# The last mode's transposed rows from products with its weights as stationary operand, and the first output units in another order

## The chip, the core and the metric

The kernel runs on one core of one Trainium2 chip. The metric is the device time of one execution in microseconds, as the median of several runs. All times inside an execution are counted from the start of the profiled span. PE is the matrix engine (its weight loads are told apart as PEld), DVE the vector engine, ACT the scalar engine, POOL and SP two further engines that here mainly issue DMAs.

## The reference, cut to what matters

```
# attention: 8 batches, 8 heads, 576 tokens, head size 64; causal window of 128 with a linear bias per head
attn = softmax(q @ k.T / 8 + bias)  (masked);   x = (attn @ v), heads side by side: [8, 576, 512]
# spectral mix, 64 modes, 512 channels
X  = rfft(x, axis=tokens)[:, :64]
Yr = Xr @ w_r[m] - Xi @ w_i[m];   Yi = Xr @ w_i[m] + Xi @ w_r[m]      # for every mode m: 512 x 512 weights
y  = irfft(Y, n=576);   u = x + y
out = u + relu(u @ w_ch)                                              # float32, [8, 576, 512]
```

The 64 pairs of 512 x 512 float32 weights are the bulk of what is read; the output is 9.4 MB.

## The kernel before, in words

The first part (up to some 138 us) is attention, done per batch and half of the heads; its output x stays on the chip, and its spectrum is laid down in XC, channels on the partitions, for each mode 32 columns (8 batches, real and imaginary parts, with signs). While it runs, and long after, POOL issues the loads of the mode weights, cast to bf16 in flight.

The second part goes through the modes as the weights come. Four modes make a group; their products (`nc.tensor.matmul(into[...], lhsT=XC[...], rhs=wq[t][a])`, L886) lie in four strips of 32 partitions of one PSUM tile, acc. The stationary operand is XC's 32 columns of a mode, the moving operand the 512 columns of its weights, and eight products make a mode: four channel quarters a for the real weights, four for the imaginary. A finished group is scaled, transposed and put into YT (`quad_end`), and YT is later turned into Z (the spectral rows per pair of batches) and ZW (the same times w_ch). In the shadow of the loads PE also projects the tokens by w_ch (XW) and adds the early modes' inverse transform (`project`, `augment`).

The last group (modes 60 to 63) is treated apart. Modes 60 to 62 go into a tile of their own, pa; `late_end` (L588 to L596) scales them into 96 rows of yq, patches those rows into Z by DMA, transposes them and puts the transposed columns into yT. Mode 63 comes last, in acc; its imaginary weights are loaded in three pieces, and PE does the real weights' four products, the transposes of the 96 rows, then the imaginary weights' four. After that stands the code that the change is about:

- ACT scales mode 63's 32 rows of acc into yq (L960), in two halves; PE transposes each half (L962), DVE copies it into yT (L964). A product of no use (L955) stands before, on PE.
- `late_channels` multiplies yT by w_ch (L601); ACT copies the result, in two halves, into yw, which lies in F's memory (L603).
- `patch` (L648) moves rows of yq into Z and of yw into ZW, one DMA per batch: for batches 0 and 1 partly on SP's queue, the others on POOL's, one after another.

Then the output is made in 18 units of two times 128 token rows (`units`; j = 0 to 3 are batches 0 and 1, j = 4 to 7 batches 2 and 3, j = 8 the last 64 tokens of batches 0 to 3, and so on). For a unit, mm gathers u @ w_ch (from XW and ZW: `begin`, `channels`), yy gathers u (from x and Z: `add_tokens`, `finish_tokens`); `activate` has ACT apply the relu to mm (L802), `finish` has DVE add yy and the relu (L842) into one of five buffers o, and SP issues the store (L844, L851). Units 1, 2 and 17 go in halves. mm and yy have two buffers each. Units 0 and 1 do not wait for patched rows of Z and ZW in all their parts: unit 0 takes the last group straight from yq and yw, through `last_rows` (L786). `with_tokens` has ACT copy unit 0's yy (L816), `finish_first` has DVE do relu and addition in one operation (L823).

The order on each engine is the order in which the code is written out: nothing is reordered by a scheduler. Waits are on other engines' counters and on DMA landings.

Of the kernel before, what the change touches and what calls it, by code (L numbers as in the profile page):

```python
# [10 lines left out]
FP32 = mybir.dt.float32  # L11
BF16 = mybir.dt.bfloat16
# [3 lines left out]
PSUM = bass.MemoryType.PSUM  # L16
# [4 lines left out]
P = 128  # L21
# [13 lines left out]
NC = 24  # L35
# [377 lines left out]
def kernel(  # L413
# [21 lines left out]
    XC = const.tile([P, 4 * NC * NM + 16 * NM], BF16, name="XC")  # L435
    ident = const.tile([P, P], BF16, name="ident")
# [24 lines left out]
    wq, homes, todo_w, again = {}, {}, [i for turn in turns for i in turn], []  # L461
# [108 lines left out]
    with ExitStack() as mctx:  # L570
# [8 lines left out]
        lctx, pctx = ExitStack(), ExitStack()  # L579
        lps = lctx.enter_context(tc.tile_pool(name="lps", bufs=1, side="right", space=PSUM))  # L580
        ps = pctx.enter_context(tc.tile_pool(name="fps", bufs=1, space=PSUM))
        heads, free, idle = {}, [], []
# [13 lines left out]
            nc.vector.tensor_copy(yT[:, :, rows], tr[:, :, rows])  # L596
            heads[LAST] = yq, yT

        def late_channels(zw, yT, yw, c):
            for et in range(4):  # L600
                nc.tensor.matmul(zw[:, c], lhsT=yT[:, et], rhs=wch[:, et, c],  # L601
                                 start=(et == 0), stop=(et == 3))
            nc.scalar.copy(yw[:, c], zw[:, c])  # L603

        def quad_end(acc, g):

# [57 lines left out]
        units = []  # L664
# [69 lines left out]
            nc.vector.tensor_copy(src[:, 1], ys[1])  # L734

        HALVES = (1, 2, len(units) - 1)
        mms, yys, rs = {}, {}, {}

        def pair(tag, slot=0):
            return heads[tag][slot].tile([P, 2, DM], FP32, tag=tag, name=tag)  # L740
# [68 lines left out]
        def finish_tokens(j):  # L809

            late_modes(yys[j][0], j, Z)

        def with_tokens(o, n):

            last_rows(yys[0][0], 0, heads["yq"], (n,))
            nc.scalar.copy(o[:, n], yys[0][0][:, n])  # L816

        def finish_first(o):

            (mm, mm_slot), (_, yy_slot) = mms.pop(0), yys[0]  # L820
            for n in range(2):
                last_rows(mm, 0, heads["yw"], (n,))
                nc.vector.scalar_tensor_tensor(out=o[:, n], in0=mm[:, n], scalar=0.0,  # L823
                                               in1=o[:, n], op0=ALU.max, op1=ALU.add)
                nc.sync.dma_start(out=out[n, :P], in_=o[:, n])
                if n == 0:
                    with_tokens(o, 1)
            del yys[0]
            idle.append(mm_slot)
            free.append(yy_slot)  # L830

        def finish(j):

            b, st = units[j]
            if j not in yys:
                take(j)
            add_tokens(j)
            finish_tokens(j)
            (yy, slot), r = yys.pop(j), rs.pop(j)
# [15 lines left out]
            free.append(slot)  # L855
# [4 lines left out]
        for g in range(NM // 4):  # L860
            if g == 0:
                lps.tile([P, 2, 4, P], BF16, tag="tr", name="tr")
            acc = (lps if g % 2 else ps).tile([P, DM], FP32, tag="acc", bufs=1, name="acc")
            if g == LAST:
                part_acc = ps.tile([P, DM], FP32, tag="pa", bufs=1, name="pa")
            for i in range(8):
                k = 8 * g + i
                if i == 6 and g == LAST:
                    pctx.close()
                    head = mctx.enter_context(  # L870
                        tc.tile_pool(name="hps", bufs=1, space=PSUM, reuse_waits="tile"))
                    heads.update(mm=[head], yy=[head])
                    idle.append(0)
                    free.append(0)
                    begin(0)
                    channels(0)
                    take(0)
                    add_tokens(0)
                    finish_tokens(0)
                now = turns.pop(0) if turns and spot[turns[0][0]] == k else []  # L880
                for a in range(4):
                    for t in now:
                        m, ri = t // 2, t % 2
                        c0 = (a // 2 * 2 * NC + 16 * (1 - ri) + a % 2 * 8) * NM + m
                        into = part_acc if g == LAST and m < NM - 1 else acc
                        nc.tensor.matmul(  # L886
                            into[32 * (m % 4) : 32 * (m % 4) + 32],
                            lhsT=XC[:, c0 : c0 + 31 * NM + 1 : NM], rhs=wq[t][a],
                            start=(ri == 0 and a == 0), stop=(ri == (m > 0) and a == 3),
                            tile_position=(0, 32 * (m % 4)),  # L890
                        )
# [7 lines left out]
                if k == K1:  # L899
# [45 lines left out]
            elif g == LAST - 1:  # L945
# [6 lines left out]
        zctx = ExitStack()  # L952
        zps = zctx.enter_context(tc.tile_pool(name="zps", bufs=1, space=PSUM))
        zl = zps.tile([P, DM], FP32, tag="z0", name="zl")
        nc.tensor.matmul(zl, lhsT=ident, rhs=wch[:, 0], start=True, stop=True)  # L955
        sides = (slice(0, DM // 2), slice(DM // 2, DM))
        trs = (lps.tile([P, 4, P], BF16, tag="tr", name="tr"),
               zps.tile([P, 4, P], BF16, tag="z1", name="tr1"))
        for i, c in enumerate(sides):
            nc.scalar.mul(yq[96:, c], acc[96:, c], 2.0 / S)  # L960
            for et in (2 * i, 2 * i + 1):
                nc.tensor.transpose(trs[i][:, et, 96:], yq[96:, et * P : (et + 1) * P],  # L962
                                    ident[96:, 96:])
            nc.vector.tensor_copy(yT[:, 2 * i : 2 * i + 2, 96:],  # L964
                                  trs[i][:, 2 * i : 2 * i + 2, 96:])
# [18 lines left out]
        begin(1)  # L984
        channels(1)
        channel_rows = partial(patch, rows=yw, dst=lambda b: ZW[:, b // 2, 1])
        channel_rows([(nc.sync, 0), (nc.sync, 1)] + [(nc.gpsimd, b) for b in range(2, B)])
        patch([(nc.gpsimd, 7)], yq, lambda b: Z[:, b // 2, 1], 6)

        assert not side  # L990
        finish_first(first)
        activate(1)
        finish(1)
        activate(2)
        for j in range(3, len(units)):
            activate(j)
            finish(j - 1)
# [31 lines left out]
```

## Time and profile before

| | us |
|---|---|
| median of 3 runs | 438.93 (438.69 to 439.68) |
| the profiled execution | 437.99 |
| its span | 436.1 |

| engine | busy, us | share of the span |
|---|---|---|
| PE | 316.2 | 73% |
| DVE | 184.5 | 42% |
| ACT | 162.3 | 37% |
| POOL | 90.2 | 21% |

The granted clock of PE was 0.862 in the mean of the span, and 1.00 from 396 to 431 us. HBM gave 162.53 MB and took 9.44 MB. The last weights' last product ended at 402.8; the first store was issued at 406.9; the DMA engines were busy with stores until 434.

How to read it: the page cuts the span into 40 slices of 10.9 us, and its DMA row gives the busy share of the 16 DMA engines in tenths. Its chain of waits lists what released what. The groups of instructions give a line, an engine, an operation, the tiles (out<-in), the shape and the mean length. The timeline gives start and length, how many instructions were merged into a row, and in brackets the idle time before it with what ended it.

### The profile page before, as it was taken

Reading aid. Unit: us, or ns where it says so; the run is one execution under the profiler, and the core shown is the slowest. Engines: PE = TensorE matmul, PEld = TensorE weight load, DVE = VectorE, ACT = ScalarE, POOL = GpSimd, SP = SyncE. Lnnn points to the kernel's source line nnn. Section 1 sums busy time; section 2 is a strip of 40 time slices with the busy share of each in tenths; the row PEclk is TensorE's granted clock in tenths of the full one; section 3 lists DMA queues with packets and bytes.
Section 4 is the critical chain, followed back from the end, with each engine's and each line's share of the span. In section 5 each row is a group of like instructions: output and inputs, shape, how many; then the busy total and the mean of one; then the engine's idle time right before and its main releaser. Section 6 shows DMA issues by size and latency. Waiting matters only on the chain.

```text
span 436.1 us, 8292 instructions
## 1 busy us (share of the span) xinstructions
PE 316.2 (73%) x3488; PEld 177.7 (41%) x3509; DVE 184.5 (42%) x332; ACT 162.3 (37%) x211; POOL 90.2 (21%) x170
## 2 busy tenths in 40 slices
PE   5589899979686635543442487999889999788982
PEld 4367677757565312111111133444434444334430
DVE  7789799887783301000000021322213233122684
ACT  6949899988681000000000011322222322102780
POOL 8701010103424002222112110101111110012600
PEclk9969999999999955555555569999999999989997
DMA  8999999999999999999999999999999999998598
GB/s 285 326 311 310 290 316 300 307 298 299 252 217 212 215 215 213 214 214 214 215 212 214 214 215 214 215 214 215 215 214 214 215 215 215 213 215 153 190 378 311
DMA packets 50453, 105.54 MB, mean 242 GB/s; under 512 B 4032, under 2 KB 21072, under 8 KB 50416
## 3 DMA queue, kind: packets, MB, share of 16 engines
q0 software_dynamic: 19440, 68.41, 77.9%
q1 hardware_dynamic: 30976, 36.60, 25.3%
q8 instruction: 27, 0.44, 0.4%
q14 instruction: 10, 0.08, 0.1%
HBM read 162.53 MB, written 9.44 MB: 394 GB/s over the span
## 4 chain that ended last, share of the span: by engine, by line
DMA 71%; PE 10%; DVE 8%; issue 5%; POOL 2%; ACT 1%; SPq 1%; DVEq 0%; POOLq 0%; ACTq 0%
DMA w<-in_moe_w_i_dram 42%; DMA wch<-in_moe_w_ch_dram 8%; DMA qr<-in_q_dram 7%; DMA vr<-in_v_dram 6%; DVE o L842 3%; DMA qr<-in_moe_w_i_dram 3%; PE my L702 2%; DMA vr<-in_moe_w_r_dram 2%; DMA kr<-in_k_dram 2%; DVE vb L246 1%; PE acc L886 1%; PE av L344 1%; POOL Z L648 1%; PE my L659 1%; DVE att L318 1%
## 5 line engine op out<-in xcount | busy, mean ns | idle before, releaser
L886 PE MATMUL acc<-w,XC 128*32 128x512 bf16 x456 | 80.3, 478 | 68.5 <-DMA w<-in_moe_w_i_dram 34.2
L886 PEld LDWEIGHTS <-XC 128*32 128x32 bf16 x508 | 38.4, 147 | 109.2 <-issue 82.8
L307 ACT ACTIVATE att<-sc 128x1024 bf16<-128x1024 f32 x64 | 64.1, 1032 | 9.7 <-PE sc L297 9.6
L636 ACT CAST ZW<-zw 128x512 bf16<-128x512 f32 x8 | 4.7, 585 | 142.9 <-PE zw L634 142.9
L344 PE MATMUL av<-vb,att 128*128 128x132 bf16 (+1 forms) x576 | 38.4, 217 | 13.3 <-DVE x L360 8.6
L344 PEld LDWEIGHTS <-att 128*128 128x128 bf16 x704 | 36.6, 98 | 18.7 <-DVE x L360 12.0
L608 DVE TENSOR_SCALAR yq<-acc 128x512 bf16<-128x512 f32 x14 | 9.6, 687 | 81.8 <-PE acc L886 81.8
L702 PE MATMUL my<-wch,xT 128*64 128x512 bf16 x288 | 34.5, 381 | 5.7 <-ACT x L733 4.2
L711 ACT CAST XW<-my 128x512 bf16<-128x512 f32 x36 | 19.3, 589 | 50.5 <-PE my L659 50.5
L683 DVE COPY xT<-tr 128x1024 bf16<-128x1024 bf16 x18 | 12.4, 692 | 54.9 <-PE tr L681 54.9
L269 ACT COPY qkT<-tp 128x1152 bf16<-128x1152 bf16 x30 | 33.5, 1116 | 4.1 <-PE tp L263 3.6
L491 POOL DMA_DIRECT2D w<-in_moe_w_r_dram x22 | 15.6, 710 | 72.1 <-PE acc L886 46.1
L491 POOL DMA_DIRECT2D w<-in_moe_w_i_dram x23 | 16.3, 709 | 64.1 <-PE acc L886 45.3
L297 PE MATMUL sc<-qkT 64*64 64x256 bf16 (+2 forms) x640 | 25.1, 263 | 4.8 <-ACT qkT L269 1.2
L360 DVE TENSOR_TENSOR x<-av,rec 128x640 bf16<-128x640 f32 x32 | 26.4, 825 | 1.1
L702 PEld LDWEIGHTS <-xT 128*64 128x64 bf16 x288 | 17.1, 109 | 21.5 <-issue 9.1
L246 DVE CAST vb<-vr 64x1024 bf16<-64x1024 f32 x32 | 22.6, 708 | 0.2
L733 ACT CAST x<-my 128x512 bf16<-128x512 f32 x18 | 10.5, 585 | 31.6 <-PE my L659 31.6
L297 PEld LDWEIGHTS <-qkT 64*64 64x64 bf16 x640 | 14.5, 109 | 19.1 <-issue 16.0
L734 DVE CAST x<-my 128x512 bf16<-128x512 f32 x18 | 12.4, 692 | 21.7 <-PE my L659 21.7
L842 DVE TENSOR_TENSOR o<-yy,r 128x1024 f32<-128x1024 f32 (+1 forms) x20 | 20.3, 1059 | 2.1 <-ACT r L802 1.9
L318 DVE TENSOR_TENSOR att<-att,mask 128x1024 bf16<-128x1024 bf16 x32 | 20.5, 682 | 0.0
(137 smaller groups left out, 424.7 us busy)
## 6 DMA issues: line engine op xcount, KB each, us to landing
w<-in_moe_w_i_dram POOLq DMA_DIRECT2D x23, 1024.0 KB, 36.2
w<-in_moe_w_r_dram POOLq DMA_DIRECT2D x22, 1024.0 KB, 35.6
qr<-in_q_dram SPq DMA_DIRECT2D x16, 576.0 KB, 7.9
kr<-in_k_dram SPq DMA_DIRECT2D x16, 576.0 KB, 7.9
w<-in_moe_w_r_dram POOLq DMA_DIRECT2D x16, 512.0 KB, 14.2
vr<-in_v_dram SPq DMA_DIRECT2D x56, 128.0 KB, 7.6
w<-in_moe_w_i_dram POOLq DMA_DIRECT2D x13, 512.0 KB, 24.0
out_dram<-o SPq DMA_DIRECT2D x13, 512.0 KB, 5.0
```

Of the source, the lines that this page charges most:

```text
L246: nc.vector.tensor_copy(self.vb[u % 2][row, :, :, :, W * half : W * half + D], src[row, :2])
L269: (self.nc.vector.tensor_copy if u < 2 and w == "q" else self.nc.scalar.copy)(dst.rearrange("q h (p j) -> q h p j", j=TPP), tp.rearrange(" ...
L297: nc.tensor.matmul(sc[64 * half : 64 * half + 64, e, j * 256 + c0 : j * 256 + c0 + n], lhsT=qkT[row, 1, h, k0 + j : k0 + P : 2], rhs=qkT[r ...
L307: self.nc.scalar.activation(self.att[u % 2][:, kt * 8 * P : (kt + 1) * 8 * P], sc.rearrange("p e n -> p (e n)"), AF.Exp, scale=1.0 / math. ...
L318: nc.vector.tensor_tensor(out=rows, in0=rows, in1=self.table[:, heads], op=ALU.mult)
L344: nc.tensor.matmul(bank[:, qt * W : qt * W + rhs[j].shape[1]], lhsT=att[:, o : o + P], rhs=rhs[j], start=(n == 0 and j == 0), stop=(n == l ...
L360: nc.vector.tensor_tensor(out=self.x[:, b, :, cs].rearrange("p t (h d) -> p h t d", h=2), in0=tiles[:, :, :, :D], in1=rec.unsqueeze(-1).br ...
L491: nc.gpsimd.dma_start(out=t.rearrange("p s a e -> p s (a e)"), in_=w[kinds.pop()][m : m + 2].rearrange("m (p a) e -> p m (a e)", a=4))
L702: nc.tensor.matmul(mm[ROWS[half]], lhsT=lhsT, rhs=wch[:, dt], start=(dt == 0), stop=False, skip_group_check=True,)
L711: nc.scalar.copy(XW[:, j, n], mms[n])
L842: nc.vector.tensor_tensor(out=o[:, c], in0=yy[:, c], in1=r[:, c], op=ALU.add)
L886: nc.tensor.matmul(into[32 * (m % 4) : 32 * (m % 4) + 32], lhsT=XC[:, c0 : c0 + 31 * NM + 1 : NM], rhs=wq[t][a], start=(ri == 0 and a == 0 ...
```

## The change

Mode 63's columns of yT are no longer transposed from acc. A new function, `last_columns`, multiplies them directly: the stationary operand is a 128 x 128 block of the mode's weights, the moving operand XC's 32 columns, and 32 such products (two kinds of weights, four quarters, four blocks) gather in a PSUM tile lastT, opened before mode 63 begins. They stand ahead of each of mode 63's products into acc, which stay, for the rows in yq. DVE scales lastT into yT. ACT scales acc into yq in one operation.

The channel products (L979 of the changed kernel) come ahead of unit 0's token products; their copies move from ACT to DVE. Unit 0's two token products and copies are done together, and ahead of unit 1's begin; `finish_first` does its channel products together. POOL's row patches are issued for two batches at a time, tokens and channels in turn. Unit 2's token products are moved ahead of unit 3's `activate` (`tokens_of`). The product of L955 is gone.

```diff
-        def late_channels(zw, yT, yw, c):
+        def last_columns(t, a):
+            m, ri = t // 2, t % 2
+            c0 = (a // 2 * 2 * NC + 16 * (1 - ri) + a % 2 * 8) * NM + m
             for et in range(4):
-                nc.tensor.matmul(zw[:, c], lhsT=yT[:, et], rhs=wch[:, et, c], ...)
-            nc.scalar.copy(yw[:, c], zw[:, c])
+                nc.tensor.matmul(
+                    lastT[:, et], lhsT=wq[t][a][:, et * P : (et + 1) * P],
+                    rhs=XC[:, c0 : c0 + 31 * NM + 1 : NM],
+                    start=(ri == 0 and a == 0 and et == 0), stop=(ri == 1 and a == 3), ...)
...
-        def with_tokens(o, n):
-            last_rows(yys[0][0], 0, heads["yq"], (n,))
-            nc.scalar.copy(o[:, n], yys[0][0][:, n])
+        def with_tokens(o):
+            last_rows(yys[0][0], 0, heads["yq"])
+            for n in range(2):
+                nc.scalar.copy(o[:, n], yys[0][0][:, n])
...
         def finish_first(o):
+            last_rows(mm, 0, heads["yw"])
             for n in range(2):
-                last_rows(mm, 0, heads["yw"], (n,))
                 nc.vector.scalar_tensor_tensor(out=o[:, n], in0=mm[:, n], ...)
                 nc.sync.dma_start(out=out[n, :P], in_=o[:, n])
-                if n == 0:
-                    with_tokens(o, 1)
...
+                    zps = zctx.enter_context(tc.tile_pool(name="zps", bufs=1, space=PSUM))
+                    lastT = zps.tile([P, 4, 32], FP32, tag="z1", name="lastT")
                     begin(0)
...
+                        if m == NM - 1:
+                            last_columns(t, a)
...
-        zl = zps.tile([P, DM], FP32, tag="z0", name="zl")
-        nc.tensor.matmul(zl, lhsT=ident, rhs=wch[:, 0], start=True, stop=True)
-        for i, c in enumerate(sides):
-            nc.scalar.mul(yq[96:, c], acc[96:, c], 2.0 / S)
-            for et in (2 * i, 2 * i + 1):
-                nc.tensor.transpose(trs[i][:, et, 96:], yq[96:, et * P : (et + 1) * P], ...)
-            nc.vector.tensor_copy(yT[:, 2 * i : 2 * i + 2, 96:], trs[i][:, 2 * i : 2 * i + 2, 96:])
+        nc.vector.tensor_scalar_mul(yT[:, :, 96:], lastT, 2.0 / S)
+        nc.scalar.mul(yq[96:], acc[96:], 2.0 / S)
         patch([(nc.sync, 0), (nc.gpsimd, 1)], yq, lambda b: Z[:, b // 2, 1])
-        patch([(nc.gpsimd, b) for b in (2, 3, 4, 5, 6)], yq, lambda b: Z[:, b // 2, 1], 6)
+        token_rows = partial(patch, rows=yq, dst=lambda b: Z[:, b // 2, 1], lo=6)
+        token_rows([(nc.gpsimd, 2), (nc.gpsimd, 3)])
...
-        with_tokens(first, 0)
         for i, c in enumerate(sides):
             zl = zps.tile([P, DM], FP32, tag=f"z{i}", name=f"zl{i}")
-            late_channels(zl, yT, yw, c)
+            for et in range(4):
+                nc.tensor.matmul(zl[:, c], lhsT=yT[:, et], rhs=wch[:, et, c], ...)
+            nc.vector.tensor_copy(yw[:, c], zl[:, c])
+        with_tokens(first)
...
-        channel_rows([(nc.sync, 0), (nc.sync, 1)] + [(nc.gpsimd, b) for b in range(2, B)])
-        patch([(nc.gpsimd, 7)], yq, lambda b: Z[:, b // 2, 1], 6)
+        channel_rows([(nc.sync, 0), (nc.sync, 1), (nc.gpsimd, 2), (nc.gpsimd, 3)])
+        for b in range(4, B, 2):
+            both = [(nc.gpsimd, b), (nc.gpsimd, b + 1)]
+            token_rows(both)
+            channel_rows(both)
...
         activate(2)
+        tokens_of(2)
         for j in range(3, len(units)):
             activate(j)
             finish(j - 1)
```

More of the change, by code (lines that the diff above doesn't have):

```diff
@@ L578 @@
         nc.gpsimd.memset(YT[:, 1, :, :, HM - 4 :], 0.0)
-        lctx, pctx = ExitStack(), ExitStack()
+        lctx, pctx, zctx = ExitStack(), ExitStack(), ExitStack()
         lps = lctx.enter_context(tc.tile_pool(name="lps", bufs=1, side="right", space=PSUM))
@@ L597, in late_end @@
             heads[LAST] = yq, yT
-        def late_channels(zw, yT, yw, c):
+        def last_columns(t, a):
+            m, ri = t // 2, t % 2
+            c0 = (a // 2 * 2 * NC + 16 * (1 - ri) + a % 2 * 8) * NM + m
             for et in range(4):
-                nc.tensor.matmul(zw[:, c], lhsT=yT[:, et], rhs=wch[:, et, c],
-                                 start=(et == 0), stop=(et == 3))
-            nc.scalar.copy(yw[:, c], zw[:, c])
+                nc.tensor.matmul(
+                    lastT[:, et], lhsT=wq[t][a][:, et * P : (et + 1) * P],
+                    rhs=XC[:, c0 : c0 + 31 * NM + 1 : NM],
+                    start=(ri == 0 and a == 0 and et == 0), stop=(ri == 1 and a == 3),
+                    skip_group_check=True,
+                )
         def quad_end(acc, g):
@@ L736 @@
         HALVES = (1, 2, len(units) - 1)
-        mms, yys, rs = {}, {}, {}
+        mms, yys, rs, summed = {}, {}, {}, set()
         def pair(tag, slot=0):
@@ L830, in finish_first, with tokens_of @@
             free.append(yy_slot)
-        def finish(j):
-            b, st = units[j]
+        def tokens_of(j):
             if j not in yys:
@@ L838, in finish @@
             finish_tokens(j)
+            summed.add(j)
+        def finish(j):
+            b, st = units[j]
+            if j not in summed:
+                tokens_of(j)
             (yy, slot), r = yys.pop(j), rs.pop(j)
@@ L951 @@
         yq, yT = heads[LAST]
-        zctx = ExitStack()
-        zps = zctx.enter_context(tc.tile_pool(name="zps", bufs=1, space=PSUM))
-        zl = zps.tile([P, DM], FP32, tag="z0", name="zl")
-        nc.tensor.matmul(zl, lhsT=ident, rhs=wch[:, 0], start=True, stop=True)
         sides = (slice(0, DM // 2), slice(DM // 2, DM))
-        trs = (lps.tile([P, 4, P], BF16, tag="tr", name="tr"),
-               zps.tile([P, 4, P], BF16, tag="z1", name="tr1"))
-        for i, c in enumerate(sides):
-            nc.scalar.mul(yq[96:, c], acc[96:, c], 2.0 / S)
-            for et in (2 * i, 2 * i + 1):
[L962 to L965, printed above, removed]
+        nc.vector.tensor_scalar_mul(yT[:, :, 96:], lastT, 2.0 / S)
+        nc.scalar.mul(yq[96:], acc[96:], 2.0 / S)
         patch([(nc.sync, 0), (nc.gpsimd, 1)], yq, lambda b: Z[:, b // 2, 1])
-        patch([(nc.gpsimd, b) for b in (2, 3, 4, 5, 6)], yq, lambda b: Z[:, b // 2, 1], 6)
+        token_rows = partial(patch, rows=yq, dst=lambda b: Z[:, b // 2, 1], lo=6)
+        token_rows([(nc.gpsimd, 2), (nc.gpsimd, 3)])
         yw = F[:, : DM // (2 * NM)].rearrange("p a b -> p (a b)")
@@ L970 @@
         first = heads["out"].tile([P, 2, DM], FP32, tag="o", bufs=5, name="o")
-        with_tokens(first, 0)
         for i, c in enumerate(sides):
             zl = zps.tile([P, DM], FP32, tag=f"z{i}", name=f"zl{i}")
-            late_channels(zl, yT, yw, c)
+            for et in range(4):
+                nc.tensor.matmul(zl[:, c], lhsT=yT[:, et], rhs=wch[:, et, c],
+                                 start=(et == 0), stop=(et == 3))
+            nc.vector.tensor_copy(yw[:, c], zl[:, c])
+        with_tokens(first)
         zctx.close()
```

## The prediction

> **What bounds the kernel now.** I read the page's slices first, then the timeline around the last weight load, then a table of 1 us stretches over the tail.
>
> ```profile
> DMA  8999999999999999999999999999999999998598
> GB/s 285 326 311 310 290 316 300 307 298 299 252 217 212 215 215 213 214 214 214 215 212 214 214 215 214 215 214 215 215 214 214 215 215 215 213 215 153 190 378 311
> ```
>
> The DMA engines are full from the first slice to the 36th: weights stream in until 402 us, and the change touches no load before the last two (real and imaginary weights of mode 63). Only the dip (slices 37, 38) and the output stream after it, at 378 GB/s, can move. Where the dip begins:
>
> ```profile
> 400.10 1.08 PE L886 MATMUL acc<-w,XC 128*32 128x512 bf16 x4
> 401.11 0.34 PE L593 MATMUL tr<-ident,yq 96*128 96x96 bf16 x4
> 401.39 0.86 PE L886 MATMUL acc<-w,XC 128*32 128x512 bf16 x3
> 402.42 0.38 PE L886 MATMUL acc<-w,XC 128*32 128x512 bf16 x1 [0.17 <-DMA w<-in_moe_w_i_dram]
> 402.88 0.65 ACT L960 ACTIVATE yq<-acc 32x256 bf16<-32x256 f32 x2 [5.04 <-PE acc L886]
> 403.56 0.51 DVE L964 COPY xT<-tr 128x64 bf16<-128x64 bf16 x2 [1.70 <-PE tr L962]
> 403.95 1.04 PE L601 MATMUL zl<-wch,xT 128*128 128x256 bf16 x8
> 404.63 0.76 ACT L603 CAST F<-zl 128x256 bf16<-128x256 f32 x2
> ```
>
> Columns: start, length, engine. See the 0.17 us: PE waited only that long for the last weights, so work put ahead of its last product has 0.17 us of cover. From the product's end (402.80) to F, the patched channel rows, ready (405.39) are 2.6 us.
>
> ```profile
> 407.00:408.00 1.00, 1.00 (x15) 0.38 (x15) 0.69 (x1) 0.51 (x2) 1.00 (x3) 1.00 0.23 72
> 408.00:409.00 1.00, 0.87 (x19) 0.42 (x15) 0.88 (x2) 1.00 (x3) 1.00 (x3) 1.00 0.83 279
> 411.00:412.00 1.00, 1.00 (x23) 0.55 (x17) 1.00 (x2) 1.00 (x2) 0.00 (x0) 1.00 0.82 284
> 412.00:413.00 1.00, 0.93 (x20) 0.52 (x16) 1.00 (x2) 1.00 (x2) 0.00 (x0) 1.00 1.02 379
> 433.00:434.00 1.00, 0.00 (x0) 0.00 (x0) 0.00 (x0) 0.00 (x0) 0.00 (x0) 0.50 0.92 348
> ```
>
> Last columns: granted clock, DMA share, GB/s. Outputs flow from 407.5; until 412 they are held to some 280, then they run full to 434. So the end is set by when the first four units are issued and how well the stream fills; later units queue behind it. The issues of before: unit 0's halves 406.89 and 407.85, unit 1's 408.84 and 409.44, unit 2's 410.51 and 411.24, unit 3 at 412.24.
>
> **The new products (L604; it, L968, L979 and L981 are lines of the changed kernel).** 32 pairs of weight load and 32-column product, four ahead of each of mode 63's eight acc products. No row has a full-array load with a 32-column product. The nearest is attention's 66-column one:
>
> ```profile
> 43.21 0.22 PE L344 MATMUL av<-vt,att 128*128 128x66 bf16 x2
> 43.27 0.22 PE L344 MATMUL av<-vb,att 128*128 128x132 bf16 x1
> ```
>
> Two pairs in 0.06: 0.03 each. The bounds: 0.013 (32 of the 66 columns' time) and 0.098 (the load's own length, below, were nothing hidden). I take 0.03. Changing the array's shape costs more: acc to acc is 0.215 in the trace, but the fourth acc (400.80) to the first transpose (401.11) 0.31, so 0.10 extra, and going back 0.09. A group then is 0.31 + 3 x 0.03 + (0.03 + 0.09) = 0.52, against 0.215. From 400.10: the fourth acc of the real weights at 400.10 + 0.21 + 3 x 0.52 = 401.87, transposes at 402.18 to 402.45, the fourth group of the imaginary weights at 402.45 + 3 x 0.52 = 404.01, its four products out at T = 404.01 + 0.09 + 0.18 (L962's length) = 404.3; acc ends at 404.6 instead of 402.80. By the bounds of the pair T is 403.8 or 406.4. The weights have landed by 402.4, so PE, not the load, now ends this stage.
>
> **From T to F.** Gone: the split scaling on ACT, four transposes, two copies, the idle product of L955. New: one scaled copy of lastT (128x128, as L409 below), eight L979 products (0.11 apart, as L601), two copies on DVE (as L408).
>
> ```profile
> L408 DVE CAST XC<-xt 128x256 bf16<-128x256 f32 x1 | 0.4, 426 | 1.8 <-ACT XC L407 1.8
> L409 DVE TENSOR_SCALAR XC<-xt 128x128 bf16<-128x128 f32 x1 | 0.3, 281 | 0.0
> L344 PEld LDWEIGHTS <-att 128*128 128x128 bf16 x704 | 36.6, 98 | 18.7 <-DVE x L360 12.0 <-DVE att L318 4.4 <-issue 1.1
> L886 PEld LDWEIGHTS <-XC 128*32 128x32 bf16 x508 | 38.4, 147 | 109.2 <-issue 82.8 <-DMA w<-in_moe_w_r_dram 17.8 <-ACT XC L407 1.6
> L193 PEld LDWEIGHTS <-F 128*32 128x32 bf16 x32 | 0.7, 96 | 0.3 <-issue 0.2
> ```
>
> T + 0.04 + 0.28 + 0.06 + 7 x 0.11 + 0.27 + 0.04 + 0.43 = T + 1.9: F at 406.2 instead of 405.39, +0.8. ACT's one scaling (0.59, as its 128x512 copies) follows acc: 405.25, hidden under L979.
>
> **First units.** PE goes L979, two yy products, unit 1's begin and channels, then the four products with F without stopping. Before, it stood 0.57 waiting for L823 (406.08 to 406.65); that wait is gone. Its end: T + 0.38 + 0.87 (L979) + 0.22 + 0.30 (yy, and the change of shape) + 0.24 + 0.32 (unit 1) + 0.65 + 0.38 (the four) = T + 3.36 = 407.66, against 407.45: ACT's relus start 0.2 later. Unit 0 needs both copies on ACT and both products: issues at 407.8 and 408.4, +0.9 and +0.55. Unit 1: +0.2. Unit 2: its token products before stood behind unit 3's mm, which waited for ACT (409.06 to 409.70); moved ahead, they leave DVE waiting only for ACT: 410.35 and 410.95, 0.15 to 0.3 earlier. Unit 3 waits for ACT's relus in series: 412.3, +0.06.
>
> **Queues.** SP's two channel patches follow F at once and are wanted some 2.1 us after it; before, they were used 2.7 after it without a wait. That bounds a wait at 0 to 0.6; I count 0.15, inside unit 2's figure. POOL still issues 13 patches of 0.51, starting at 405.5 instead of 403.81, ending near 412.2. Unit 4's channel rows come fourth and fifth, at 407.05 and 407.6 against 406.85 and 407.42, land 2.1 to 2.4 later, and are wanted near 410.2: covered by 0.2, and by no more than unit 4's slack if the landing is later. The last pairs are wanted after 420.
>
> **Sum.** The end moves between unit 3's +0.06 and unit 0's +0.9. Before, the stream had moved 938 KB by 411.0 of the 1048 KB issued by 410.3: it had little queued, so units 1 to 3 (+0.2, -0.2, +0.06) weigh more than unit 0. I take +0.3. On the profiled execution: 437.99 + 0.3 = 438.3; that run lies 0.94 below the median of the runs, which I move by the same: 439.2. This kernel's runs spread by 0.2%, 0.9 us, so the forecast is no change that can be told.
>
> **A rule against it.** The row above says 0.03 a pair. The Trainium skill, TensorE: Matmul & The Clock Gate, section LDWEIGHTS (loading the stationary operand), has a load take its columns over 1.2 GHz: by estimate 107 ns for 128, and unhidden behind so short a product the 32 pairs would cost 2.5 us more than I count. The 66-column row of this trace speaks against that.
>
> **The rivals.**
> - Loads not hidden (6%). A pair costs the load's 0.098 since a 32-column product is too short to cover it: 32 x 0.068 = 2.2 later, 439.2 + 2.2 = 441.4. Against it: the 66-column pairs.
> - The moving operand is slow (20%). L604 reads XC as moving operand, 64 elements apart. As stationary operand that costs: L886's loads take 147 ns, L193's, same shape but contiguous, 96. Were the 0.05 paid per pair, 32 x 0.05 = 1.6 later: 440.8. It decides slower from a pair of about 0.05 on, where 0.6 is added to 0.3. For it: the two load rows. Against: no product row with such a step.
> - The stream fills better (14%). Between 408 and 412 it lost (4 x 379 - 279 - 282 - 305 - 284) / 379 = 1 us, with row patches landing among it. With the patches in pairs and unit 2 earlier, that us could be regained while unit 3 stays put: 438.9 - 1.0 = 437.9. It decides where the stream runs at over 370 GB/s from 409 to 412. Against: as many patches, later, still beside the outputs, and a later first output.
> - It does nothing (15%): unit 3 alone decides and stays put: 439.0.
>
> **Numbers.** My case has 45%: 439.2. With the last rival and most of it within 0.9 us, 57% no change; 14% faster by more; 29% slower (20, 6 and 3 of my own upper end, where unit 0 decides). The range takes in the slow moving operand and the fuller stream: 437.9 to 440.8.
>
> **What would show it.** acc ending near 404.6, lastT's copy near 404.3, F near 406.2, PE unbroken to 407.7, first output issue near 407.8, unit 2's before 410.6, unit 3's at 412.3, the stream full to 434.4. acc ending after 405.5 means dear pairs; 370 GB/s before 411 with an end before 433.5, the third rival. Wrong altogether if the granted clock falls under 1.00 or unit 4 waits for its patches by over 0.5.

## The result: 441.62 us, slower by 0.65%, and the profile after

| | before, us | after, us |
|---|---|---|
| median of 6 runs each | 438.81 (438.23 to 439.68) | 441.62 (441.24 to 442.82) |
| the profiled execution | 437.99 | 441.24 |
| its span | 436.1 | 439.3 |

The ratio is 1.0065, with a 95% interval from 1.0045 to 1.0084: some 2.8 us, where 0.3 had been forecast.

Part of the difference of the two profiled executions is not of the change. The last weights (imaginary, mode 63) landed at 402.37 us in the one and at 403.36 in the other, and over the twelve traces of this study that landing lies anywhere from 401.83 to 406.57, though no kernel differs from another much before it. So I count from the landing of the last weights. From there to the end of the span it is 33.7 us before and 36.0 after: 2.26 us more. That is what has to be explained. (The medians lie 2.81 apart; with one trace of each kernel, where the other 0.55 comes from stays open.)

The page's slices after, the same two rows as before:

```profile
DMA  8999999999999999999999999999999999996598
GB/s 285 329 317 307 286 304 300 305 295 294 247 214 213 214 214 214 213 213 214 215 214 213 215 213 214 214 215 214 215 214 214 214 213 215 214 214 115 189 367 317
```

Nothing moved in the first 36 slices. The 37th fell from 153 to 115 GB/s: the dip between the last weights and the outputs has become longer. The stretches of 1 us (columns as in the prediction; granted clock, DMA share and GB/s last) show where it ends:

```profile
410.00:411.00 1.00, 0.82 (x12) 0.21 (x8) 0.84 (x2) 1.00 (x2) 1.00 (x3) 1.00 0.10 26
411.00:412.00 1.00, 1.00 (x19) 0.46 (x20) 0.89 (x2) 0.19 (x2) 1.00 (x2) 1.00 0.81 284
417.00:418.00 1.00, 1.00 (x8) 0.31 (x4) 1.00 (x2) 0.53 (x1) 0.00 (x0) 1.00 1.03 379
437.00:438.00 1.00, 0.00 (x0) 0.00 (x0) 0.00 (x0) 0.00 (x0) 0.00 (x0) 0.50 0.45 168
```

The clock is still 1.00. Outputs begin to flow after 411 instead of after 407.5, the stream first reaches 379 GB/s in 417 instead of in 412, and it ends in 437 instead of 434. The timeline shows what came late:

```profile
401.76 0.22 PEld L604 LDWEIGHTS <-w 128*128 128x128 bf16 x4 [0.23 <-issue]
401.77 0.39 PE L604 MATMUL lastT<-XC,w 128*128 128x32 bf16 x4
402.09 0.43 PE L901 MATMUL acc<-w,XC 128*32 128x512 bf16 x1
402.45 0.39 PE L604 MATMUL lastT<-XC,w 128*128 128x32 bf16 x4
406.53 0.29 DVE L968 TENSOR_SCALAR xT<-lastT 128x128 bf16<-128x128 f32 x1 [1.98 <-PE lastT L604]
406.88 1.05 PE L979 MATMUL zl<-wch,xT 128*128 128x256 bf16 x8
407.53 0.86 DVE L981 CAST F<-zl 128x256 bf16<-128x256 f32 x2 [0.71 <-PE zl L979]
408.85 1.04 PE L792 MATMUL mm<-F,FM 128*128 128x512 bf16 x4
```

See the distance from one row of lastT to the next: 402.45 - 401.77 = 0.68 for four pairs and one acc product, where 0.52 was counted. Each row of loads stands behind 0.23 of "issue", which is time in which the profile shows nothing that was waited for. The imaginary weights are not waited for: they landed by 403.36, and PE comes to them at 404.00. (The first load of all, at 401.09, names the DMA of the real weights, behind the same 0.41 of idle time that stands at this place in the kernel before.) The last lastT product is out at T = 406.43, F is ready at 408.39.

With the four stretches that follow one another, the prediction can be held against the two traces:

| stretch, us | before | predicted | after |
|---|---|---|---|
| first product of mode 63 to T (before: to the end of acc) | 2.69 | 4.20 | 5.34 |
| from there to F ready | 2.60 | 1.9 | 1.96 |
| F ready to the issue of unit 3 | 6.85 | 6.1 | 6.98 |
| issue of unit 3 to the end of the span | 23.84 | 24.1 | 23.96 |
| sum | 35.98 | 36.3 | 38.24 |

The second and the fourth came as forecast. The first is short by 1.14, the third by 0.88. (Unit 3's issue: 412.24 before, 415.37 after.) Against the kernel before, the loss is in the first stretch, 2.65 us, of which the second gives 0.64 back. The third was to become 0.75 shorter, and became 0.13 longer.

### The profile page after: what moved, and what is told of

Same layout as the page of the kernel before. It is cut to its first block, busy times and chain, and to the rows that moved or that the text cites. A ratio compares the mean times of both kernels' runs of the same rounds, so it can differ in the third digit from the quotient of the medians.

```text
span 439.3 us, 8362 instructions
## 1 busy us (share of the span) xinstructions
PE 323.4 (74%) x3536; PEld 179.9 (41%) x3536; DVE 185.4 (42%) x333; ACT 161.4 (37%) x208; POOL 90.2 (21%) x170
## 4 chain that ended last, share of the span: by engine, by line
DMA 71%; PE 12%; DVE 8%; ACT 3%; issue 3%; POOL 0%; SPq 0%; DVEq 0%; ACTq 0%; POOLq 0%
DMA w<-in_moe_w_i_dram 46%; DMA w<-in_moe_w_r_dram 11%; DMA kr<-in_k_dram 7%; DMA qr<-in_q_dram 4%; PE av L344 2%; PE acc L901 2%; DVE vb L246 2%; ACT att L307 1%; DVE x L360 1%; DVE att L318 1%; DMA vr<-in_v_dram 1%; DMA out_dram<-o 1%; DVE o L853 1%; PE tp L263 1%; DVE k L251 1%
## 5 line engine op out<-in xcount | busy, mean ns | idle before, releaser
L901 PE MATMUL acc<-w,XC 128*32 128x512 bf16 x456 | 81.9, 488 | 66.1 <-DMA w<-in_moe_w_i_dram 33.4
L284 PE MATMUL sc<-bias,ident 128*128 128x512 bf16 x64 | 21.2, 416 | 1.1 <-ACT att L307 1.1
```

What stands on the lines that cost most here:

```text
L284: nc.tensor.matmul(sc[:, e], lhsT=self.ident, rhs=self.bias[:, hv].rearrange("p j n -> p (j n)"), start=True, stop=False, skip_group_check ...
L901: nc.tensor.matmul(into[32 * (m % 4) : 32 * (m % 4) + 32], lhsT=XC[:, c0 : c0 + 31 * NM + 1 : NM], rhs=wq[t][a], start=(ri == 0 and a == 0 ...
```

## The experiments

The table puts them together. All times but the median count from the landing of the last weights, in the profiled execution of each kernel; "unit 0" is the issue of its second half.

| kernel | T | unit 0 | unit 3 | end | median, us | ratio to before |
|---|---|---|---|---|---|---|
| before | | 5.48 | 9.87 | 33.71 | 438.81 | |
| after | 3.07 | 7.51 | 12.01 | 35.97 | 441.62 | 1.0065 [1.0045, 1.0084] |
| e1 columns only | 3.08 | 9.79 | 14.17 | 37.96 | 442.30 | 1.0076 [1.0049, 1.0104] |
| e2 order only | | 5.53 | 10.31 | 34.24 | 438.68 | 1.0001 [0.9987, 1.0014] |
| e3 contiguous | 2.07 | 6.50 | 11.49 | 35.14 | 439.02 (one run) | |
| e4 blocked | 0.99 | 5.92 | 10.95 | 34.93 | 439.38 | 1.0011 [0.9986, 1.0035] |
| e5 fetch moved | 3.36 | 7.80 | 12.30 | 36.43 | 441.31 | 1.0078 [1.0049, 1.0107] |
| e7 unit 2 early | | 5.48 | 9.76 | 34.09 | 438.41 | 0.9997 [0.9969, 1.0026] |
| e8 copied and blocked | 0.31 | 5.24 | 10.70 | 34.54 | 438.73 | 1.0006 [0.9988, 1.0024] |
| e9 unit 3 in halves | | 5.47 | 9.40 | 34.05 | 438.94 | 1.0013 [0.9991, 1.0036] |
| e10 copied, blocked, fetch moved | 0.32 | 5.24 | 9.73 | 34.02 | 438.60 | 1.0007 [0.9993, 1.0021] |
| e11 before, fetch moved | | 5.48 | 9.87 | 33.97 | 439.09 | 1.0023 [0.9996, 1.0051] |

e1 to e4, e5 to e9, and e10 with e11 were each timed beside the kernel before (its medians 438.42, 438.95 and 438.20), so ratios are compared, not medians across these three.

### e1 and e2: the two halves of the change, each by itself

e1 is the kernel before with lastT alone; e2 is the kernel after with the transposes put back.

```diff
 e1, against before
+                        if m == NM - 1:
+                            last_columns(t, a)
...
+        nc.vector.tensor_scalar_mul(yT[:, :, 96:], lastT, 2.0 / S)
+        nc.scalar.mul(yq[96:], acc[96:], 2.0 / S)
-        (the scaling in halves, the transposes, the copies to yT, L955)

 e2, against after
-                        if m == NM - 1:
-                            last_columns(t, a)
...
+        (the scaling in halves, the transposes, the copies to yT, L955)
-        nc.vector.tensor_scalar_mul(yT[:, :, 96:], lastT, 2.0 / S)
-        nc.scalar.mul(yq[96:], acc[96:], 2.0 / S)
```

> Only the new products: lastT replaces the transposes of mode 63's rows, all else as before (unit 0's token product still ahead of the channel products, copies on ACT, patches in the old order). Measured by the stretch from the landing of the last weights to the end of the span: 33.7 us before, 35.9 after. Theory 1, the new products on PE cost the time: mode 63's acc ends some 3.4 us after the last landing as in the changed kernel, and the stretch is 35.9 or, since the old order puts a wait for acc's scaling ahead of the channel products, up to 37. Theory 2, the new order costs it: 33.7 to 34.5, and the time within 0.2% of before.

> Only the new order: mode 63's columns by transposes as before, the rest as in the changed kernel. Theory 1: the stretch is 33.0 to 33.9 and the time within 0.2% of before or a little faster. Theory 2: 35 to 36, and slower by 0.4% or more.

By the medians e2 is at the level of before, e1 at that of after or above. So the loss comes with the new products, and the new order by itself neither costs nor brings anything that can be told. In the profiles both end a little later than expected (34.24, where up to 33.9 was expected, and 37.96, where it was up to 37). In e2 unit 1's first half is issued 0.33 earlier than in before (6.13 after the landing for 6.46), but unit 3 is 0.44 later. The timeline shows why:

```profile
407.96 0.41 PE L756 MATMUL mm<-XW,ident 64*64 64x512 bf16 x4 [0.46 <-DVE o L818]
408.17 0.94 PE L653 MATMUL mm<-ZW,FT 64*64 64x512 bf16 x4
409.15 2.00 ACT L796 ACTIVATE r<-mm 128x512 f32<-128x512 f32 x3 [1.09 <-PE mm L653]
```

Unit 2's begin waits 0.46 for DVE's relu of unit 0, which has to leave its PSUM tile first. Then its four ZW products take 0.94 instead of 0.41. The trace names no releaser for the stop among them, but batch 1's patched rows, which they read, come late (the packets of its patch moved at 407.94 to 408.04, 0.5 later than in before). And ACT, which in before went from unit 1's relus to unit 2's without a stop, stands 1.09.

e1 is dearer than the whole change in the profile (37.96 against 35.97). In the old order PE comes to unit 0's first token product before the channel products, and that product waits for ACT's scaling of acc, which is now the last thing to be ready:

```profile
405.99 0.59 ACT L970 ACTIVATE yq<-acc 32x512 bf16<-32x512 f32 x1 [8.11 <-DVE xT L969]
406.63 0.59 PE L798 MATMUL yy<-yq,FM 128*128 128x512 bf16 x1 [0.73 <-ACT yq L970]
407.01 1.92 PE L601 MATMUL zl<-wch,xT 128*128 128x256 bf16 x8
408.96 0.37 ACT L603 CAST F<-zl 128x256 bf16<-128x256 f32 x1 [0.44 <-PE zl L601]
```

lastT is out at 405.54, and F only at 409.33, 3.8 later, against 1.96 in the kernel after; besides the later start, the channel products are spread over 1.92 instead of 1.05. With T at the same 3.08 after the landing, unit 3 stands at 14.17 in e1 and at 12.01 in after: it is the new order that lets the columns from lastT be used.

### e3 and e4: what the products cost

e3 reads 32 neighbouring columns of XC as moving operand instead of 32 that lie 64 elements apart (so lastT holds other modes' columns). e4 puts each half's 16 pairs in one block ahead of its four acc products.

```diff
 e3
-                    rhs=XC[:, c0 : c0 + 31 * NM + 1 : NM],
+                    rhs=XC[:, c0 : c0 + 32],
 e4
-                        if m == NM - 1:
-                            last_columns(t, a)
+                        if m == NM - 1 and a == 0:
+                            for block in range(4):
+                                last_columns(t, block)
```

> The changed kernel with 32 neighbouring columns of XC as moving operand of the new products, in place of columns 64 elements apart: lastT is another matrix, the work is the same in kind and count. If the step of the moving operand sets the pair, it falls from 0.058 us to 0.03, a group from 0.68 to 0.59, and the stretch from 35.9 to some 35.2. If the weight load sets it, pair, group and stretch stay.

> The changed kernel with the sixteen new products of one kind of weights in one block, ahead of its four acc products: two changes of the array's shape for each kind instead of eight. If the change of shape is what makes a group 0.68 us, mode 63 takes 8 x 0.68 - 6 x 0.25 = 3.9 in place of 5.4, and the stretch is some 34.5. If a pair simply takes long wherever it stands, it stays near 35.9.

The timelines, of e3 first:

```profile
400.25 0.27 PE L604 MATMUL lastT<-XC,w 128*128 128x32 bf16 x4
400.44 0.43 PE L901 MATMUL acc<-w,XC 128*32 128x512 bf16 x1
400.81 0.27 PE L604 MATMUL lastT<-XC,w 128*128 128x32 bf16 x4
```

and of e4:

```profile
402.35 1.08 PE L604 MATMUL lastT<-XC,w 128*128 128x32 bf16 x16
403.36 1.08 PE L902 MATMUL acc<-w,XC 128*32 128x512 bf16 x4
404.37 0.34 PE L593 MATMUL tr<-ident,yq 96*128 96x96 bf16 x4
404.55 1.09 PE L604 MATMUL lastT<-XC,w 128*128 128x32 bf16 x16
```

In e3 a group takes 400.81 - 400.25 = 0.56 instead of 0.68; inside it the products start 0.026 apart instead of 0.058. The step of the moving operand thus costs 0.12 a group, and 8 x 0.12 = 0.96 of T; measured, the stretch to T fell from 5.34 to 4.37. What is left of the group, 0.56 - 0.215 for acc alone - 4 x 0.026 = 0.24, is the change of the array's shape there and back.

In e4 the sixteen pairs take 403.36 - 402.35 = 1.01 with one change of shape, the four acc products 1.01 with the other: 2.02 for a half, where four groups of 0.68 take 2.72. That is 0.23 for each of the three pairs of changes left out, the same number from another side. T is 2.1 earlier than after, partly from this, and partly because the four acc products of the imaginary half now come behind it. e4's ratio to before, 1.0011 against the 1.0065 of after, with intervals that do not meet, says without the profile that blocking wins most of the loss back; e3 has one run.

The end of e3 came as expected (35.14 for 35.2), that of e4 0.4 later than expected. Unit 3 did not come forward with T in either: T is 1.0 earlier in e3 and unit 3 only 0.52; in e4 2.08 and 1.06. In both the first token patch after the scaling took 2.83 and 2.72 from issue to landing, which leads to the next experiment.

### e5: the transfer that the chain of waits names

The chain of waits of the kernel after has these pieces (start, length, what):

```profile
406.88 0.60 ACT yq L969
407.48 0.28 issue
407.76 2.81 DMA Z<-yq
410.57 0.04 issue
410.61 0.41 PE yy L665 x2
```

POOL's first token patch took 2.81 from issue to landing, against 1.71 in before, and PE stood 0.18 for it. The trace shows beside it a transfer of another kind: an instruction fetch, one packet of 16 KB, 0.96 us long, from 408.58 on. In e3 the two can be seen to collide: the fetch lasts from 406.15 to 407.17, 14 of the 16 packets of the two first patches move at 406.50 to 406.65, and the last two, of 1 KB each, at 407.17 and 407.22, as it ends. In the kernel after it is less plain: all sixteen had moved by 409.03, only a few packets of 4 bytes stand at the fetch's end (409.53 to 409.56), and the landing is told at 410.57. Over the twelve traces these fetches stand 165 to 344 of PE's recorded instructions apart, 256 in the median. So they should move if PE gets more instructions ahead of them:

```diff
             for _ in range(3):
                 wt = ps.tile([P, DM], FP32, tag="my", bufs=2, name="my")
                 nc.tensor.matmul(wt, lhsT=ident, rhs=wch[:, 0], start=True, stop=True)
+            for _ in range(12):
+                nc.tensor.matmul(wt[:, :32], lhsT=ident, rhs=wch[:, 0, :32], start=True, stop=True)
```

> The changed kernel with twelve 32-column products more in each of the six warming calls, long before the last mode's weights: 144 TensorE instructions more, so that TensorE's 16 KB instruction fetch, which stood at 408.58 beside the token patch of POOL in the changed kernel, comes about half a fetch interval earlier. Theory A (the lastT products and their array changes alone cost the time): nothing changes, the stretch from the landing of the last weights to the end of the span stays 35.9 +- 0.3, the median 441.6, whatever the patch takes. Theory B (the fetch holds the patch up, and TensorE's stops for Z and ZW behind it cost 0.2 to 0.45): the patch lands in 1.6 to 1.8 instead of 2.81, the 0.18 wait of unit 1's second Z products is gone, unit 3 is issued 0.2 to 0.45 earlier relative to the landing (11.6 to 11.8 instead of 12.01), the stretch 35.5, the median 441.2.

The fetch went to 399.41, the patch landed in 1.72, the wait for Z was gone, and nothing was won: unit 3 stands 8.94 after T, to the hundredth what it was. Another wait had stood right behind the one named. Of e5:

```profile
408.31 1.29 DVE L832 SCALAR_TENSOR_TENSOR o<-mm,o 128x512 f32<-128x512 f32 x2 [1.17 <-ACT o L825]
409.65 0.41 PE L770 MATMUL mm<-XW,ident 64*64 64x512 bf16 x4 [0.46 <-DVE o L832]
```

PE, no longer held by Z, waits 0.46 for DVE to leave unit 0's PSUM tile. In the kernel after, that relu ended at 410.84 and unit 2's begin started at 410.89: it would not have been earlier without the patch's delay. The gain that theory B expected does not come. (The end, at 36.43, is also later than theory A's 35.9 +- 0.3: PE came to mode 63 1.98 ahead of the landing instead of 2.27, with the fetch now just before it.)

### e8 and e10: both costs taken away

e8 copies mode 63's columns to a contiguous tile XM early and blocks the products; e10 moves the fetch as well.

```diff
+                    XM = right.tile([P, 2, 56], BF16, name="XM")
+                    for h in range(2):
+                        o = 2 * h * NC * NM + NM - 1
+                        nc.vector.tensor_copy(XM[:, h], XC[:, o : o + 55 * NM + 1 : NM])
...
-            c0 = (a // 2 * 2 * NC + 16 * (1 - ri) + a % 2 * 8) * NM + m
+            c0 = 16 * (1 - ri) + a % 2 * 8
...
-                    rhs=XC[:, c0 : c0 + 31 * NM + 1 : NM],
+                    rhs=XM[:, a // 2, c0 : c0 + 32],
...
-                        if m == NM - 1:
-                            last_columns(t, a)
+                        if m == NM - 1 and a == 0:
+                            for block in range(4):
+                                last_columns(t, block)
```

> The changed kernel, with both costs of the new products taken away as far as they go: mode 63's 2 x 56 columns of XC are copied by VectorE to a contiguous tile some hundred us earlier and serve as moving operand, and the 16 products of each half come in one block ahead of its four acc products (two changes of shape per half instead of eight). Theory 1: pairs 0.026 apart (as with contiguous columns), each half 16 x 0.026 + 0.16 + 4 x 0.215 + 0.3 = 1.7 instead of 2.9; T 1.9 to 2.3 earlier relative to the landing than in the changed kernel (+0.8 to +1.2 instead of +3.07), unit 3 at +10.0 to +10.4, the stretch 33.7 to 34.2, the median 438.0 to 439.0: the level of before or a little under it. Rival (the order or the patches keep what the products lose): the stretch stays over 34.7 with T early.

T came 0.31 after the landing, earlier than expected: PE now waits for the weights again (0.21). The median, 438.73, lies where theory 1 has it. In the profile unit 3 and the end were later than theory 1 has them, 10.70 and 34.54; the rival was right in that the patches keep a part, if not as much as it said. Of e8:

```profile
402.68 0.27 PE L604 MATMUL lastT<-XM,w 128*128 128x32 bf16 x4 [0.21 <-DMA w<-in_moe_w_i_dram]
406.82 0.41 PE L768 MATMUL yy<-x,ident 64*64 64x512 bf16 x4
408.31 0.41 PE L665 MATMUL yy<-Z,FT 64*64 64x512 bf16 x4 [1.08 <-DMA Z<-yq]
```

Here the fetch (at 405.69, 1.20 long) holds the first token patch for 3.15 from issue to landing, and now nothing stands behind it: PE loses 1.08. So the fetch, whose delay of the patch gained nothing when it was taken away from the kernel after, costs 1 us of PE's time here, and e10 was made to take it away.

> Copied columns and blocks, as before, and the twelve 32-column products more in each warming call. In the kernel with copied columns and blocks the instruction fetch stood at 405.69, the first token patch took 3.15 from issue to landing, and TensorE stood 1.08 waiting for Z (DMA Z<-yq) in unit 1's token products; unit 3 was issued 5.46 after unit 0's second half, against 4.39 in the kernel before and 4.50 in the changed one. Theory 1 (with the products cheap, the fetch is what is left): the patch lands in 1.6 to 1.8, the 1.08 wait is gone, unit 3 follows unit 0's second half by 4.4 to 4.6 and stands near +9.7 after the landing of the last weights, the stretch is 33.4 to 33.8, the median 0.5 to 1.1 under that of copied columns and blocks: a ratio to before of 0.998 to 0.9995. Rival (another wait takes its place, as in the changed kernel itself, where moving the fetch moved nothing): unit 3 still 5.2 or more after unit 0's second half, the median unchanged at 438.7.

```profile
407.35 0.41 PE L770 MATMUL yy<-x,ident 64*64 64x512 bf16 x4
407.59 0.39 PE L665 MATMUL yy<-Z,FT 64*64 64x512 bf16 x4
408.43 0.41 PE L770 MATMUL mm<-XW,ident 64*64 64x512 bf16 x4 [0.45 <-DVE o L832]
```

The wait for Z is gone, the patch lands in 1.70, unit 3 follows unit 0 by 4.49 and stands at 9.73, as expected, and PE is back at the wait for DVE. The end (34.02) is 0.2 later than the expected 33.4 to 33.8. In the medians the expected gain of 0.5 to 1.1 is not there: the ratio to before is 1.0007, for 1.0006 in e8 and an expected 0.998 to 0.9995. So what gave 0.97 at unit 3 and 0.52 at the end, in one trace each, is nothing that the medians can tell (their intervals reach 0.6 to 0.8 us to either side), and the kernel is at the level of before. It is the change with both costs paid off, and it has nothing to show over before: unit 0 is 0.24 earlier, unit 3 only 0.14, the end not at all. e3's and e4's first patches took 2.83 and 2.72, for the 3.15 of e8; whether the fetch is what held unit 3 there was not tried.

> The kernel before with the same products more in the warming calls, as a control: the fetch stood at 409.72 there, among output transfers and row patches, and no wait of TensorE named a patch. Theory 1: unit 3 still 4.3 to 4.5 after unit 0's second half, the median within 0.4 of before. Rival (the extra products or the moved fetch change the time by themselves): over 0.5 to either side, and the gain or loss of the run beside it would be the fetch's alone.

The control stands where before does in the profile (9.87 and 33.97); its median is 0.9 higher, more than the 0.4 that theory 1 allows, with an interval that still holds 1. So moving the fetch gains before nothing, and whether the products added to warm() have a small price of their own (which e10 would then pay too) stays open.

### e7 and e9: unit 3 and the stream

e7 is before with `tokens_of(2)` ahead of unit 3's begin; e9 adds unit 3 to those that are issued in halves. (`tokens_of` is defined in both as in the changed kernel.)

```diff
 e7
         activate(2)
+        tokens_of(2)
         for j in range(3, len(units)):
 e9
-        HALVES = (1, 2, len(units) - 1)
+        HALVES = (1, 2, 3, len(units) - 1)
```

> The kernel before, with one part of the new order alone: unit 2's token products go ahead of unit 3's begin. From the six traces so far the span ends 23.65 to 23.98 after unit 3's issue. Theory 1 (unit 3's issue sets the end): unit 2's first half is issued some 0.6 earlier (near 409.9 in a run whose last weights land at 402.37), but unit 3's only 0.0 to 0.25 earlier since its relu follows two others on ACT in series; the median is 0.0 to 0.25 lower, no change that can be told. Rival (unit 2 counts as much as unit 3, since the stream has little queued then): 0.3 to 0.6 lower.

> The kernel before with unit 2's token products early and unit 3 also relued, added and issued in two halves. Theory 1 in its strict form (the end follows the moment from which the stream always has work queued, which is unit 3's issue): unit 3's first half goes out 0.5 to 0.6 earlier, its second half 0.1 later at most; the end is 0.2 to 0.5 earlier than with unit 2 early alone, the median 437.9 to 438.4 where before has 438.4 to 438.9. Rival (the stream is held by the transfers beside it or by the total bytes, not by issues): no change within 0.1%.

In e7 unit 2's first half is issued 0.48 earlier than in before (7.66 after the landing for 8.14), its second half 0.42 later, and unit 3 0.11 earlier; the median did not move (ratio 0.9997). Unit 3's 0.11 is theory 1's figure, but the interval of the median, some 1.2 us to either side, can't tell the two theories apart. In e9 unit 3's first half is 0.5 earlier and the end no earlier than e7's (34.05 for 34.09; the ends of before and e11, whose tails are alike, differ by 0.26). So in these traces the strict form fails: it is not the first piece of unit 3 that counts. Where unit 3 is issued whole, its issue and the end lie 23.65 to 24.33 apart in eleven traces, while the issue itself moves over 4.4 us (9.73 to 14.17); in e9 it is 24.65 from the first half and 24.12 from the second.

## Why the prediction was wrong

**The pair (counted 0.03).** It is 0.058. I took it from attention's 66-column product, whose moving operand is contiguous; with contiguous columns it is indeed 0.026 (e3). The second rival, the slow moving operand, was the right mechanism, and its price of 0.05 on every pair was too high (0.032 measured); it had 20%, since no row showed a product with such a step. The Trainium skill has the rule that I should have weighed there: SBUF — State Buffer, section Door 1: The DMA port swizzle, says that SBUF is read in lines of 16 bytes and that a bf16 operand can be strided for free only over 8 elements. XC's columns lie 64 apart, and the traces agree in direction; the price, 0.058 against 0.026, is theirs. Of the 0.16 by which a group came out longer than counted, the four pairs make 0.11.

**The change of shape (counted 0.10 and 0.09).** It is 0.24 there and back, 0.05 of the 0.16. Pair and change of shape together are the first step that failed. Over seven groups ahead of T the two terms together make 7 x (0.68 - 0.52) = 1.12, and T came 1.14 late. The sign that I named, acc ending after 405.5, was there: it ended at 406.79, 405.80 on the clock of before's landing.

**Loads not hidden (6%, 441.4).** The time came out near this rival's, for another reason. The loads of L604 take 95 to 117 ns each (95 to 100 in e3), and yet the products start 26 ns apart in e3: they are hidden. The rule of the Trainium skill that the prediction cites (107 ns for a load) is near their length and says nothing of their pitch; a second one on that page of the Trainium skill, section Wait — 56ns, not 53.3ns?, puts the floor between small products at about 25 ns, and e3's 26 agrees.

**The stream fills better (14%).** It did not: from 411 to 417 it ran at 281 to 349 GB/s.

**From T to F, and PE unbroken to the four F products.** Right: F at T + 1.96 for T + 1.9, the end of the products at T + 3.45 for T + 3.36.

**Unit 0 (407.8 and 408.4, or T + 3.5 and T + 4.1).** Issued at T + 3.84 and T + 4.43, 0.3 late: DVE's first relu starts at T + 3.12, released by ACT's copies of yy (1.17 <-ACT o L823), and the two, of 0.69 each, run in series.

**Unit 3 waits for ACT's relus in series (+0.06).** This is the second step that failed. Of the kernel before:

```profile
407.13 0.69 DVE L823 SCALAR_TENSOR_TENSOR o<-mm,o 128x512 f32<-128x512 f32 x1 [0.54 <-PE mm L786]
407.49 6.90 ACT L802 ACTIVATE r<-mm 128x512 f32<-128x512 f32 x9 [0.79 <-PE mm L786]
407.87 0.41 PE L762 MATMUL mm<-XW,ident 64*64 64x512 bf16 x4
```

and of the kernel after:

```profile
409.55 1.29 DVE L830 SCALAR_TENSOR_TENSOR o<-mm,o 128x512 f32<-128x512 f32 x2 [1.17 <-ACT o L823]
410.89 0.41 PE L768 MATMUL mm<-XW,ident 64*64 64x512 bf16 x4
411.11 0.67 PE L665 MATMUL mm<-ZW,FT 64*64 64x512 bf16 x4
411.81 1.08 ACT L808 ACTIVATE r<-mm 128x512 f32<-128x512 f32 x2 [0.81 <-PE mm L665]
```

In before ACT's relus do run without a stop. In the new order ACT stands 0.81 ahead of unit 2's relus, because unit 2's begin needs the PSUM tile that unit 0's second relu leaves on DVE: in before that tile came free at 407.82 and PE was there at 407.87, in after at 410.84 and 410.89. Unit 3 then follows that release by 4.4 to 4.5 in both. So unit 3 could not stay put while unit 0 moved by 0.55, as I had it: it goes with unit 0. With T + 8.94 for the forecast T + 8.0 this step is worth 0.9; 0.26 of ACT's 0.81 is the late patch of the next paragraph, of which 0.15 had been counted. The wait for the tile is read from the traces (0.46 and 0.45 `<-DVE o` in e2, e5 and e10); no run gave mm another tile, so what it is worth by itself was not tested.

**SP's two channel patches (0.15).** They do not follow F at once: the patch writes rows of ZW that unit 1's channel products read, and in the new order those products end later than F. It was issued at 408.94, as they ended (408.92), 0.55 after F, against 0.22 in before, and PE lost 0.26 in unit 2's ZW products (0.67 for 0.41), 0.11 over what I counted.

**Unit 4's rows, the clock, the queues.** As forecast: no wait of unit 4 for its patches shows, and the clock is 1.00.

**The sum.** The two failed steps make 1.14 + 0.88 = 2.0 of the 2.26 that the profile shows over before, and the forecast's own 0.3 the rest. They are not added costs of one kind: against before the first is time lost, the second a gain that did not come. That units 1 to 3 weigh more than unit 0 fits the distance to the end, which varies by 0.7 from unit 3's issue and by 1.1 from unit 0's over the eleven traces; the two issues mostly move together, so it is no strong test. The range ended at 440.8: it held one of the two errors, not both.

## What to carry to other kernels

A small product is priced from a row with the same step of the moving operand, or with twice the price; where a copy can make it contiguous ahead of time, and where small products can stand in one block instead of between others of another shape, most of the cost goes (here 2.72 to 1.5 us for a half). When a unit's start is moved, look for everything that hands back a buffer behind it: a PSUM tile that is released late moves units that seem to be bound by another engine. And the releaser that a chain of waits names can have a second one within 0.1 us behind it: look for when everything else that the instruction needs came free (here the tile, at 410.84), and test by taking the first one away.

## What the runs showed of the hardware that was not expected

- A 16 KB instruction fetch is one packet of 0.88 to 1.33 us (once 1.80) in the twelve traces, and a row patch that meets it lands in 2.7 to 3.15 instead of 1.5 to 1.7. It moves with PE's instruction count: 72 tiny products with their loads, added some way ahead, brought it forward from 408.58 to 399.41. It cost 1.08 of PE's time in e8; in after, moving it gained nothing.
- Four 128 x 128 loads, each shown as 95 to 117 ns, take 0.21 to 0.22 us together (L604).
- A product with 128 rows of contraction and 32 columns costs 26 ns with contiguous columns (e3) and 58 ns with columns 128 bytes apart (after); the stationary loads beside it lengthen too (median 106 ns against 96).
